# Row corrections of the last four token tiles: from a selecting matmul to rows of x, with the reloads and the tail in another order

## The chip, the cores and the metric

The kernel runs on one core of one Trainium2 chip. The metric is device time in microseconds (us), taken as the median over runs. A profiled execution gives a trace; its span runs from the first to the last instruction of the program, and times inside it are counted from its start.

## The reference

Three things are added for an input x of 2048 tokens by 512 channels, all of them on or from the layer-normed x:

```python
xn = _layernorm(x, axis=-1)
return x + A(xn) + B(xn)

# A: a long convolution, one kernel K of length 2048 per channel
P = exp(dt*A * l);  K = einsum("dn,dnl,dn->dl", C, P, dt*B).real
y = irfft(rfft(xn, 4096) * rfft(K, 4096))[:2048] + xn * Dskip
# B: a gated MLP, 512 -> 1792 -> 512
h = sigmoid(xn @ w_gate) * (xn @ w_up);  return h @ w_down
```

## The kernel before

Channels lie in two halves of 256 (p = 0 and 1), tokens in 16 tiles of 128 rows (i = 0 to 15). The MLP takes four groups of four tiles; jj is the tile in its group, so group 3 holds tiles 12 to 15. The convolution is worked on a 64 by 32 grid: forward transforms, a product per channel and frequency (VectorE, L916 and L920), a back transform (TensorE, L935) whose result V is evacuated by ScalarE (L288) and stored to HBM in the scratch tensors v_scr. After that V is needed in another layout, so it is read back: `reload` has three parts. Part 0 (the first half of the channels, v_scr_99 in the rows of the order, `v_scr0` in the code) comes in four pieces of 512 KB; part 1 (v_scr_100, three quarters of the second half) in four pieces of 384 KB; part 2 (v_scr_101, the last quarter) in four pieces of 128 KB, of which the odd ones go out on ScalarE's DMA queue and the others on SyncE's:

```python
ld = dma("ACT" if n == 2 and k % 2 else "SP", dst, v_v[:, :, w * k:w * (k + 1), :], ...)
```

Piece k serves tiles 4k to 4k+3, that is the tile pairs t = 2k and 2k+1. The last transform, `s2_mm` (L994), takes V to tokens: two column halves of two row halves for each tile, so eight matmuls of 256 columns for a pair and four for a tile.

The tail has two kinds of work. `final(t)`, t = 0 to 5, is for the tiles of the groups 0 to 2, whose MLP and x are already summed: eight matmuls into a pair of PSUM banks, then one VectorE addition of 1024 columns (L1020) and a store. The tiles of group 3 do it in one accumulation: 14 matmuls of the down projection (L1123) into a bank, then the four of `s2_mm` into the same bank, then VectorE adds x from the tile xt (L1143) and the row is stored. The last tile is cut in two column pieces of 256.

The convolution's grid leaves eight late output rows (rows 95 and 127 of the tiles 12 to 15) that lack a term. It is worked out as eight rows of 512 (`f_rz` on VectorE, four transposing matmuls L964, an evacuation by ScalarE at L966 into `rr`) and added by a fifth matmul per tile, L997, with a table of ones, `sr`, that puts each row of `rr` on its place. The other 120 rows of `rr` are set to zero by GpSimd (L854), and `sr` is loaded from a constant (c_SR).

All instructions are recorded as operations and issued in the order of one long list of numbers, `ORDER`; each engine and each DMA queue runs its own in that order, and one that waits holds up all behind it on that engine. SyncE issues nearly all the transfers, ScalarE a few. In the list, 817 to 820, 821 to 824 and 825 to 828 are the four pieces of the parts 0, 1 and 2; 829 + 3t is the matmuls of `final(t)`, 830 + 3t its addition and 831 + 3t its store.

Of the kernel before, what the change touches and what calls it, by code (L numbers as in the profile page):

```python
# [20 lines left out]
D = 512  # L21
# [161 lines left out]
def _consts():  # L183
    S1 = _build_S1()
    M2 = _build_M2()
    MA, MB = _build_MAB()
    by = np.arange(NU).reshape(2, NU // 2).T.reshape(NU)

    def quads(m, cross=False):
        m = m.transpose(1, 0, 2)  # L190
        lo, hi = m[0:64, :, 0:64].copy(), m[64:128, :, 64:128].copy()
        if cross:
            lo[:, 1::2], hi[:, 1::2] = m[64:128, 1::2, 64:128], m[0:64, 1::2, 0:64]
        return np.concatenate([lo, hi], axis=0)

    f = lambda v: np.ascontiguousarray(v.astype(np.float32)).astype(ml_dtypes.bfloat16)
    sr = np.zeros((128, 4, 64))
    for q in range(8):
        sr[q, q // 2, 31 + 32 * ((q ^ (q // 2)) % 2)] = 1.0
    return dict(SR=f(sr), ident=f(np.eye(128)), S1=f(np.tile(S1, (4, 1))), S2=f(np.stack([_build_S2(by), np.roll(_build_S2(by), 32, axis=1)], axis=1)), M2=f(quads(M2[by])),  # L200
                MAB=f(np.stack([quads(MA[by], True), quads(MB[by], True)], axis=2)), E=f(_build_E(M2, by).reshape(128, NU // 2, 2, NKT, 128).transpose(1, 0, 2, 3, 4)))
# [117 lines left out]
def kernel(  # L319
# [25 lines left out]
    def bank(slot, r=0):  # L345
        if slot.pool == "s":
            return pairs[slot.idx][:, 512 * r:512 * r + 512]
        return banks[slot.idx][:]
# [53 lines left out]
    sr = at(OFF["tmp"] + 3 * KB // 2, [4, 64])  # L402
# [449 lines left out]
    l_sr = load("SP", sr, cten["SR"].ap(), 64 * KB, deps=table_free, pkt=512)  # L852
    l_s2 = load("SP", s2, cten["S2"].ap(), 32 * KB, deps=table_free, pkt=256)
    m_rr = pl.add("POOL", 0.3, lambda: P.memset(rr, 0.0), table_free, 60)  # L854
# [97 lines left out]
    def f_rz():  # L952
        ka, kb_ = k2[:, 0:KT].unsqueeze(2), k2[:, KT:2 * KT].unsqueeze(2)
        V.tensor_tensor(out=rf[:, :, 0:4], in0=pre[:], in1=kb_.to_broadcast([128, KT, 4]), op=ALU.mult)
        V.tensor_tensor(out=rf[:, :, 4:6], in0=pre2[:], in1=ka.to_broadcast([128, KT, 2]), op=ALU.mult)
        V.tensor_tensor(out=rz[:, :, 4:8:2], in0=pre[:, :, 0:2], in1=ka.to_broadcast([128, KT, 2]), op=ALU.mult)
        V.tensor_copy(out=rz[:, :, 1:4:2], in_=rf[:, :, 0:2])
        V.tensor_tensor(out=rz[:, :, 5:8:2], in0=rf[:, :, 2:4], in1=rf[:, :, 4:6], op=ALU.add)
# [7 lines left out]
    o_rz = pl.add("ACT", 0.48, lambda slr=slr: S.activation(out=rr[0:8, :], in_=bank(slr)[0:8, :], func=ACT.Identity), [o_rt, l_sr, m_rr], 60, rel=[slr])  # L966
# [21 lines left out]
    def s2_mm(t, r, o, start, w):  # L988
# [7 lines left out]
        if i >= 12:  # L996
            T.matmul(o[64:128, :], sr[:, i - 12, :], rr[:, w[0]:w[1]], start=False, tile_position=(0, 64), **kw)  # L997
# [27 lines left out]
    for grp in range(4):  # L1025
# [77 lines left out]
        for jj in range(4):  # L1103
# [3 lines left out]
            if jj == 0:  # L1107
                if late:
                    xt = at(TAIL["xt"], [4, D])
                    lx = [dma("SP", xt, xv[:, i:i + 4, :], deps=[prods[0]] + table_free, prio=3,  # L1110
                              pkt=4096)(512 * KB)]
            last = late and jj == 3
# [3 lines left out]
            ver = vp_op[i // 2] + [l_s2, o_rz]  # L1116
# [96 lines left out]
```

## Time and profile before

| | |
|---|---|
| median of 3 runs | 214.91 us (214.5 to 215.3) |
| profiled execution, span | 213.6 us |
| median less that span | 1.3 us |
| busy: TensorE, VectorE, ScalarE, GpSimd | 204.2, 191.3, 177.1, 27.8 us |
| granted TensorE clock | 1.000 |
| HBM read, written | 24.99 MB, 12.85 MB |

No device time of its own is shown for the profiled execution beside its span, so durations of the trace are set against the 213.6 us, and the 1.3 us that lie around it go unchanged to the median. In the rows below PE is TensorE, DVE VectorE, ACT ScalarE, POOL GpSimd and SP SyncE; a q behind an engine marks what its sequencer issues, a DMA for instance. "big" is the one SBUF tile in which most buffers lie, pair and bank are PSUM. A row of the timeline gives start, length, engine, line, operation, output and inputs, shape and count, and in brackets the idle time ahead and what ended it. Some matmul records are missing (a down projection of 14 stands with 13 in one row).

### The profile page before, as it was taken

The page shows a single profiled execution, that of the slowest core. Times are in us where ns is not written, and L with a number is a line of the kernel's source. Part 1 is how long each engine was busy: PE and PEld are TensorE (multiplying, and loading weights), DVE is VectorE, ACT ScalarE, POOL GpSimd, SP SyncE. Part 2 cuts the span into 40 slices and gives each one's busy share as a digit, 9 for nine tenths or more (in the row PEclk, how much of TensorE's full clock was granted, in tenths as well). Part 3 has the DMA queues.
Part 4 walks back from the last instruction along what each step waited for, and adds up shares of the span by engine and source line. Part 5 has one row for each costly group of instructions (what it writes and reads, how often), then busy time and mean ns, then how long its engine had stood idle before and what let it go on. Part 6 is the DMA issues. An engine that isn't in the chain of part 4 may idle for free.

```text
span 213.6 us, 4875 instructions
## 1 busy us (share of the span) xinstructions
PE 204.2 (96%) x1838; PEld 102.9 (48%) x1864; DVE 191.3 (90%) x406; ACT 177.1 (83%) x284; POOL 27.8 (13%) x32
## 2 busy tenths in 40 slices
PE   7989999999999999999999999999999999999992
PEld 2654444444443444445436555544654645644482
DVE  4799999999979999999999999999992999990494
ACT  5699999999999999997999989978989998870000
POOL 2120026008980000002000000001200000000000
PEclk9999999999999999999999999999999999999999
DMA  5999269124464236967965878787967799698864
GB/s 148 316 383 381 100 147 324 61 98 147 110 126 104 76 105 229 213 191 151 249 185 141 228 202 237 215 221 175 202 188 208 217 284 274 141 357 218 240 213 172
DMA packets 52377, 42.61 MB, mean 199 GB/s; under 512 B 16641, under 2 KB 44546, under 8 KB 52354
## 3 DMA queue, kind: packets, MB, share of 16 engines
q1 hardware_dynamic: 50658, 40.30, 63.9%
q0 software_dynamic: 864, 1.57, 4.8%
q10 hardware_dynamic: 832, 0.43, 0.8%
q8 instruction: 14, 0.23, 0.5%
q14 instruction: 9, 0.07, 0.1%
HBM read 24.99 MB, written 12.85 MB: 177 GB/s over the span
## 4 chain that ended last, share of the span: by engine, by line
PE 41%; DVE 40%; POOL 6%; DMA 4%; issue 4%; ACT 3%; DVEq 0%; SPq 0%; ACTq 0%
PE pair L911 8%; PE bank L1045 7%; PE bank L1123 7%; PE bank L1069 7%; DVE big L737 6%; DVE big L738 6%; POOL ln_ve_b L481 5%; PE pair L935 5%; DVE big L742 4%; DVE big L743 4%; DVE stats L542 3%; DVE hT_sb L1094 3%; DVE hT_sb L1089 3%; DVE big L678 2%; DMA big<-v_scr 2%
## 5 line engine op out<-in xcount | busy, mean ns | idle before, releaser
L288 ACT ACTIVATE big<-pair 128x1024 bf16<-128x1024 f32 x64 | 64.5, 1039 | 6.9 <-DVE big L920 1.7
L1069 PE MATMUL bank<-xnT,wu_sb 128*128 128x512 bf16 x214 | 52.9, 379 | 1.7 <-issue 0.6
L1123 PE MATMUL bank<-wd_sb,hT_sb 128*128 128x512 bf16 (+1 forms) x231 | 50.6, 367 | 0.5 <-issue 0.2
L1045 PE MATMUL bank<-xnT,wg_sb 128*128 128x512 bf16 (+1 forms) x191 | 45.6, 370 | 1.0 <-issue 0.5
L1045 PEld LDWEIGHTS <-wg_sb 128*128 128x128 bf16 x240 | 22.5, 98 | 25.0 <-issue 3.2
L1123 PEld LDWEIGHTS <-hT_sb 128*128 128x128 bf16 x238 | 22.4, 98 | 24.9 <-issue 1.6
L1069 PEld LDWEIGHTS <-wu_sb 128*128 128x128 bf16 x224 | 20.7, 98 | 27.5 <-issue 5.4
L1057 ACT ACTIVATE hT_sb<-bank 128x512 bf16<-128x512 f32 x48 | 28.2, 627 | 0.7 <-PE bank L1045 0.7
L737 DVE TENSOR_TENSOR big<-big 128x1024 bf16<-128x1024 bf16 (+4 forms) x40 | 26.7, 667 | 0.2
L738 DVE TENSOR_TENSOR big<-big 128x1024 bf16<-128x1024 bf16 (+4 forms) x40 | 26.5, 663 | 0.0
L1084 ACT ACTIVATE us_sb<-bank 128x512 bf16<-128x512 f32 x40 | 23.6, 616 | 0.6 <-DVE hT_sb L1089 0.3
L911 PE MATMUL pair<-big 128*128 128x256 bf16 x160 | 19.8, 273 | 0.0
L916 DVE TENSOR_TENSOR big<-big 128x2048 bf16<-128x2048 bf16 x16 | 19.3, 1217 | 0.1
L911 PEld LDWEIGHTS <-big 128*128 128x128 bf16 x160 | 15.4, 98 | 4.7 <-issue 0.8
L481 POOL TENSOR_SCALAR ln_ve_b<-mvb 128x4 bf16<-128x4 bf16 x3 | 13.0, 4323 | 34.1 <-DVE mvb L543 34.1
L742 DVE TENSOR_TENSOR big<-big 128x512 bf16<-128x512 bf16 (+4 forms) x40 | 16.5, 413 | 0.2
L743 DVE TENSOR_TENSOR big<-big 128x512 bf16<-128x512 bf16 (+4 forms) x40 | 16.5, 412 | 0.0
L792 ACT ACTIVATE sq_sb<-big 128x256 bf16<-128x256 bf16 (+2 forms) x20 | 13.2, 658 | 1.6 <-DVE big L743 1.5
L1089 DVE TENSOR_TENSOR hT_sb<-hT_sb,us_sb 128x1024 bf16<-128x1024 bf16 x20 | 13.5, 683 | 0.0
L935 PE MATMUL pair<-big 64*64 64x512 bf16 (+1 forms) x256 | 13.1, 327 | 0.0
L898 DVE COPY big<-big 32x1024 bf16<-32x1024 bf16 x20 | 8.4, 418 | 4.5 <-ACT big L288 4.2
L288 ACT ACTIVATE big<-big 128x256 bf16<-128x256 bf16 x30 | 12.4, 452 | 0.0
(99 smaller groups left out, 229.8 us busy)
## 6 DMA issues: line engine op xcount, KB each, us to landing
big<-c_E SPq DMA_DIRECT2D x13, 320.0 KB, 4.4
z_scr<-big SPq DMA_DIRECT2D x16, 256.0 KB, 2.9
big<-z_scr SPq DMA_DIRECT2D x16, 256.0 KB, 4.2
v_scr<-big SPq DMA_DIRECT2D x16, 256.0 KB, 3.2
big<-big SPq DMA_DIRECT2D x44, 64.0 KB, 3.3
big<-in_A_u_dram SPq DMA_DIRECT2D x4, 512.0 KB, 9.1
wu_sb<-in_B_w_up_dram SPq DMA_DIRECT2D x2, 896.0 KB, 10.8
wd_sb<-in_B_w_down_dram SPq DMA_DIRECT2D x1, 1792.0 KB, 9.0
```

Of the source, the lines that this page charges most:

```text
L288: nc.scalar.activation(out=get(out), in_=get(in_), func=ACT.Identity)
L481: P.tensor_scalar(out=q["ve_b"], in0=mvb[:, s, 1], scalar1=EPS, scalar2=None, op0=ALU.add)
L737: V.tensor_tensor(out=wide(outp), in0=wide(lo), in1=mre, op=ALU.mult)
L738: V.tensor_tensor(out=wide(tb()), in0=wide(lo), in1=mim, op=ALU.mult)
L742: V.tensor_tensor(out=outp[:, :, 0], in0=outp[:, :, 0], in1=tb()[:, :, 1], op=opr)
L743: V.tensor_tensor(out=outp[:, :, 1], in0=outp[:, :, 1], in1=tb()[:, :, 0], op=opi)
L911: T.matmul(two(sk)[:, o:o + DW], es()[:, g, kt, :], kTv[p][:, :, kt, :], start=kt in (0, NKT - 1), stop=kt >= NKT - 2)
L935: T.matmul(two(sv)[o:o + 64, DW * (2 * g + y):2 * DW * (g + 1)], mab[b:b + 64, 2 * u + g, q, :], pq()[b:b + 64, q, ch] if y else pp()[b:b ...
L1045: T.matmul(bank(sl, k % 2)[:, c0:c1], w[:, kt, k * 128:(k + 1) * 128], xnT[:, grp, kt, c0:c1], start=(kt == 0), stop=(kt == KT - 1))
L1057: S.activation(out=hT_sb[:, hs.idx, k % 2, :], in_=bank(sl), func=ACT.Sigmoid)
L1069: T.matmul(bank(sl), wu_sb[:, kt, k * 128:(k + 1) * 128], xnT[:, grp, kt, :], start=(kt == 0), stop=(kt == KT - 1))
L1123: T.matmul(bank(po)[:, 0:c[1] - c[0]], hT_sb[:, hts[k // 2].idx, k % 2, jj * 128:(jj + 1) * 128], wd_sb[:, k, c[0]:c[1]], start=first and ...
```

## The change

The eight corrections no longer go through TensorE at the end. The eight rows of x concerned are loaded beside (x8, two transfers of 4 KB), VectorE adds them to the corrections as it evacuates them into `rr` (in ScalarE's place), and two transfers of 4 KB on ScalarE's queue write the sums over the same rows of xt, after xt itself has landed. The matmul L997, the table `sr` with its 64 KB load, and the memset of `rr` go. The columns of `rz` are numbered otherwise, to suit the two transfers. `ORDER` is another list from its second half on:

```diff
-    l_sr = load("SP", sr, cten["SR"].ap(), 64 * KB, deps=table_free, pkt=512)
+    l_x8 = [load("SP", x8[b:8:2, :], xv[95 + 32 * b, 12:16, :], 4 * KB, deps=table_free, pkt=1024) for b in range(2)]
     l_s2 = load("SP", s2, cten["S2"].ap(), 32 * KB, deps=table_free, pkt=256)
-    m_rr = pl.add("POOL", 0.3, lambda: P.memset(rr, 0.0), table_free, 60)
...
-    o_rz = pl.add("ACT", 0.48, lambda slr=slr: S.activation(out=rr[0:8, :], in_=bank(slr)[0:8, :], func=ACT.Identity), [o_rt, l_sr, m_rr], 60, rel=[slr])
+    o_rz = pl.add("DVE", 0.61, lambda slr=slr: V.tensor_tensor(out=rr[0:8, :], in0=bank(slr)[0:8, :], in1=x8[0:8, :], op=ALU.add), [o_rt] + l_x8, 60, rel=[slr])
...
-        if i >= 12:
-            T.matmul(o[64:128, :], sr[:, i - 12, :], rr[:, w[0]:w[1]], start=False, tile_position=(0, 64), **kw)
...
                     lx = [dma("SP", xt, xv[:, i:i + 4, :], deps=[prods[0]] + table_free, prio=3,
                               pkt=4096)(512 * KB)]
+                    lx = [dma("ACT", xt[95 + 32 * b:96 + 32 * b, :, :], rr[b:8:2, :], deps=lx + [o_rz], prio=3, pkt=1024)(4 * KB) for b in range(2)]
...
-            ver = vp_op[i // 2] + [l_s2, o_rz]
+            ver = vp_op[i // 2] + [l_s2]
```

Three places show how the list moves the tail. First SyncE's queue, from its last loads of the table E on. v_scr_99, _100 and _101 are the parts 0, 1 and 2 of V: an arrow from them is a reload, an arrow to them a store; the 128x2048 from in_A_u_dram is xt. Before:

```order
L422 DMA k_93<-c_scr 128x8x1
L422 DMA v_scr_100<-big 128x4x256
L422 DMA big<-in_A_u_dram 128x2048
L422 DMA big<-v_scr_99 128x2x1024
L422 DMA xnT<-v_scr_99 128x2x1024
L422 DMA v_scr_101<-big 128x4x256 x2
L422 DMA big<-v_scr_100 96x2x1024
L422 DMA big<-v_scr_101 32x2x1024
L422 DMA big<-v_scr_100 96x2x1024 x3
L422 DMA out_dram<-big 128x1024
```

Now:

```order
L421 DMA k_93<-c_scr 128x8x1
L421 DMA xnT<-v_scr_99 128x2x1024
L421 DMA v_scr_100<-big 128x4x256 x2
L421 DMA big<-v_scr_99 128x2x1024
L421 DMA big<-in_A_u_dram 128x2048
L421 DMA v_scr_101<-big 128x4x256 x2
L421 DMA big<-v_scr_100 96x2x1024 x3
L421 DMA big<-v_scr_101 32x2x1024 x2
L421 DMA big<-v_scr_100 96x2x1024
L421 DMA out_dram<-big 128x1024 x4
```

A reload of part 0 stands ahead of two stores of part 1, and the load of xt behind them; three reloads of part 1 stand ahead of those of part 2, which have to wait for the two stores of part 2 just above. By the list, the first of the three is now piece 1, then 3, then 0; before it was 0, and behind the reload of part 2's piece 0 came 3, 1 and 2.

Second the end of ScalarE's list, whose DMAs are the pieces 3 and 1 of part 2, in this order before and now. Before:

```order
L1057 ACTIVATE hT_sb<-bank_67 128x512
L966 ACTIVATE big<-pair_63 8x512
L422 DMA big<-v_scr_101 32x2x1024 x2
L422 DMA out_dram<-big 128x256
L1209 UNCONDITIONAL_BRANCH
```

Now:

```order
L1053 ACTIVATE hT_sb<-bank_68 128x512
L287 ACTIVATE big<-pair_63 128x1024
L421 DMA big<-v_scr_101 32x2x1024 x2
L421 DMA big<-big 1x4x512 x2
L421 DMA out_dram<-big 128x256
```

The evacuation of the eight rows has left ScalarE, and the two row transfers into xt stand behind the two reloads.

Third TensorE after the down projections of jj = 0 and 1 (banks 68 and 67). A pair is a `final`; rows that repeat are left out. Before, the finals are those of t = 1 and then t = 0:

```order
L994 MATMUL pair_63<-big 64x256
...
L1123 MATMUL bank_65<-wd_sb,hT_sb 128x512
...
L994 MATMUL bank_68<-big 64x256
...
L997 MATMUL bank_68<-big 64x512
...
L994 MATMUL bank_67<-big 64x256
```

Now they are t = 3 and then t = 2:

```order
L992 MATMUL pair_63<-big 64x256
...
L992 MATMUL bank_68<-big 64x256
...
L992 MATMUL bank_67<-big 64x256
...
L1120 MATMUL bank_66<-wd_sb,hT_sb 128x512
...
L992 MATMUL bank_66<-big 64x256
```

The last transform of jj = 0 and 1 stands ahead of the down projection of jj = 2 (bank 65 before, bank 66 now) and no longer behind it. VectorE's additions keep their sequence of shapes: two of 1024, three of 512, two of 1024, one of 256, two of 1024, one of 256; the first two now serve t = 3 and 2, the next two t = 1 and 0, the last two t = 5 and 4.

More of the change, by code (lines that the diff above doesn't have):

```diff
@@ L196, in _consts @@
     f = lambda v: np.ascontiguousarray(v.astype(np.float32)).astype(ml_dtypes.bfloat16)
[L197 to L200, printed above, removed]
+    return dict(ident=f(np.eye(128)), S1=f(np.tile(S1, (4, 1))), S2=f(np.stack([_build_S2(by), np.roll(_build_S2(by), 32, axis=1)], axis=1)), M2=f(quads(M2[by])),
                 MAB=f(np.stack([quads(MA[by], True), quads(MB[by], True)], axis=2)), E=f(_build_E(M2, by).reshape(128, NU // 2, 2, NKT, 128).transpose(1, 0, 2, 3, 4)))
@@ L401 @@
     rr = at(OFF["tmp"] + KB // 2, [D])
-    sr = at(OFF["tmp"] + 3 * KB // 2, [4, 64])
+    x8 = at(OFF["tmp"] + 2 * KB, [D])
     W = [at(OFF["W%d" % p], [12, 2, DW]) for p in range(NP)]
@@ L955, in f_rz @@
         V.tensor_tensor(out=rf[:, :, 4:6], in0=pre2[:], in1=ka.to_broadcast([128, KT, 2]), op=ALU.mult)
-        V.tensor_tensor(out=rz[:, :, 4:8:2], in0=pre[:, :, 0:2], in1=ka.to_broadcast([128, KT, 2]), op=ALU.mult)
-        V.tensor_copy(out=rz[:, :, 1:4:2], in_=rf[:, :, 0:2])
-        V.tensor_tensor(out=rz[:, :, 5:8:2], in0=rf[:, :, 2:4], in1=rf[:, :, 4:6], op=ALU.add)
+        V.tensor_tensor(out=rz[:, :, 4:8:3], in0=pre[:, :, 0:2], in1=ka.to_broadcast([128, KT, 2]), op=ALU.mult)
+        V.tensor_copy(out=rz[:, :, 1:3], in_=rf[:, :, 0:2])
+        V.tensor_tensor(out=rz[:, :, 5:7], in0=rf[:, :, 2:4], in1=rf[:, :, 4:6], op=ALU.add)
     o_rz = pl.add("DVE", 0.95, f_rz, [k_l, o_pre], 60)
```

82 rows, old and new, of the table ORDER are left out of this document.

## The prediction

> **What bounds the kernel now.** I began with the page: how long the span is, where VectorE and the DMA engines stand in its 40 slices (5.34 us each), and how the chain that ended last is shared out.
>
> ```profile
> span 213.6 us, 4875 instructions
> DVE  4799999999979999999999999999992999990494
> DMA  5999269124464236967965878787967799698864
> PE 41%; DVE 40%; POOL 6%; DMA 4%; issue 4%; ACT 3%; DVEq 0%; SPq 0%; ACTq 0%
> ```
>
> VectorE is full almost everywhere up to slice 35 and has one hole near the end, the digits 0 and 4. The chain spends only 4% on DMA, so one should see where. The chain of waits over the last 28 us (start, length, what):
>
> ```profile
> 191.27 2.59 DMA v_scr<-big
> ...
> 193.92 4.70 DMA big<-v_scr
> ...
> 198.67 0.95 PE pair L994 x14
> 199.62 0.16 issue
> 199.78 2.97 PE bank L1123 x13
> 202.75 0.44 PE bank L994 x5
> 203.20 0.12 PE bank L997
> 203.32 0.02 issue
> 203.34 0.69 DVE big L1143
> ...
> 204.60 0.52 DVE big L1143
> ```
>
> The last store of part 2 of V, then its reload (825, piece 0), then at 198.67 the finals of t = 1 and 0 on TensorE, then the down projection of jj = 2, and from 203.34 VectorE to the end. The timeline of VectorE shows the hole itself:
>
> ```profile
> 190.86 1.87 DVE L1094 TENSOR_TENSOR hT_sb<-hT_sb,bank 128x512 bf16<-128x512 bf16 x3
> 199.23 2.36 DVE L1020 TENSOR_TENSOR big<-pair,glu_sb 128x1024 bf16<-128x1024 f32 x2 [6.50 <-PE pair L994]
> 203.34 1.94 DVE L1143 TENSOR_TENSOR big<-bank,big 128x512 bf16<-128x512 f32 x3 [1.76 <-PE bank L997]
> 205.20 2.34 DVE L1020 TENSOR_TENSOR big<-pair,glu_sb 128x1024 bf16<-128x1024 f32 x2
> 207.47 0.41 DVE L1143 TENSOR_TENSOR big<-bank,big 128x256 bf16<-128x256 f32 x1
> 207.80 2.34 DVE L1020 TENSOR_TENSOR big<-pair,big 128x1024 bf16<-128x1024 f32 x2
> 210.06 0.41 DVE L1143 TENSOR_TENSOR big<-bank,big 128x256 bf16<-128x256 f32 x1
> ```
>
> VectorE waits 6.50 us for the first final and 1.76 us for the first tile of group 3, and then works without a gap to 210.47. So the end is set by the moment S at which the first final finds all its pieces (198.67), by the hole of 1.76, and by a fixed rest. TensorE's timeline says what it had before S:
>
> ```profile
> 197.13 1.03 PE L1123 MATMUL bank<-wd_sb,hT_sb 128*128 128x512 bf16 x4
> 198.09 0.30 PE L994 MATMUL pair<-xnT,big 128*64 128x256 bf16 x2
> 198.67 0.30 PE L994 MATMUL pair<-big 128*64 128x256 bf16 x2 [0.28 <-DMA big<-v_scr]
> ```
>
> The down projections of jj = 0 and 1 end at 198.1 to 198.2, so TensorE itself could begin at 198.2 and the reload costs half a microsecond. The transfers around it, by issue (the queue of ScalarE sends two reloads, 828 and then 826; the three rows behind it are its first, its second and SyncE's 825; then SyncE's first of 384 KB and its last two), KB each and us to landing:
>
> ```profile
> 194.01 1.43 ACTq L422 DMA_DIRECT2D big<-v_scr  x2
> ...
> big<-v_scr ACTq DMA_DIRECT2D x1, 128.0 KB, 4.8
> ...
> big<-v_scr ACTq DMA_DIRECT2D x1, 128.0 KB, 5.6
> ...
> big<-v_scr SPq DMA_DIRECT2D x1, 128.0 KB, 4.7
> ...
> big<-v_scr SPq DMA_DIRECT2D x1, 384.0 KB, 4.3
> ...
> big<-v_scr SPq DMA_DIRECT2D x2, 384.0 KB, 7.1
> ```
>
> **The change part by part.** The order decides most. The first finals are now t = 3 and 2, which read piece 1. Its last quarter is 826, the second reload on ScalarE's queue. That queue still waits for both stores of part 2, so the issue stays where it was: 194.01 for 828, half of 1.43 us later, 194.7, for 826. Before, 826 landed 5.6 us later, at 200.3, and nobody needed it then. Now TensorE stands at it, and with it everything behind in its list.
>
> *After S.* Call S' the first matmul that needs 826. VectorE starts 0.56 us behind it (198.67 to 199.23) and does two additions of 1024 in 2.36 us: free at S' + 2.92. Before, it then waited for jj = 0, whose transform stood behind the down projection of jj = 2. Now the transforms of jj = 0 and 1 stand ahead of it. The 16 matmuls of two finals take 0.95 us, so these eight take about 0.48; they are done by S' + 1.5, and VectorE goes on at once with two additions of 0.65 (1.94 / 3): busy to S' + 4.2. TensorE goes on with the down projection of jj = 2 (0.16 + 2.97) and its four matmuls with the handing over (0.44 + 0.02): 0.95 + 0.48 + 3.13 + 0.46 = S' + 5.02. There the third addition starts. Before, it started at 204.60, that is S + 5.93, and from it on both kernels have the same shapes on VectorE. Gain of the order: 5.93 - 5.02 = 0.91 us, call it 0.9; the hole shrinks from 1.76 to 0.8. The L997 matmuls that go are in this figure (0.12 on the chain).
>
> *S' itself.* If 826 lands as before, S' is 200.31 + 0.05 = 200.36: +1.69 us. The nearest rows bound it: no earlier than TensorE is free, 198.2 (-0.47); no later than the longest reload here, 7.1 us, from 194.7: 201.8 (+3.2). Two things pull. Three reloads of 384 KB now go ahead of the stores' landing, where one went: more is in the queue before 826. But the engines also had room:
>
> ```profile
> 194.00:196.00 2.00, 2.00 (x11) 0.87 (x9) 0.00 (x0) 0.00 (x0) 0.00 (x0) 1.00 0.70 210
> 196.00:198.60 2.60, 2.39 (x12) 0.89 (x10) 0.00 (x0) 0.00 (x0) 0.00 (x0) 1.00 0.93 240
> ```
>
> (stretch, its length, busy time of TensorE, weight loads, VectorE, ScalarE and GpSimd, clock, DMA share, GB/s.) In the two microseconds behind the stores the share is 0.70; the new order fills them with work that before was done later. And what stood right beside 826, the second reload of 384 KB, has moved ahead of it, not vanished. I take 200.3, the old landing, with up to 1.5 us on top in the rival below.
>
> *The row transfers.* Their price isn't in the trace; the nearest rows are a small transfer to HBM, the load of xt, which they follow, and the two stores of part 2, ahead of which xt is now issued:
>
> ```profile
> c_scr<-k_scr SPq DMA_DIRECT2D x1, 1.0 KB, 4.8
> ...
> big<-in_A_u_dram SPq DMA_DIRECT2D x1, 512.0 KB, 5.7
> ...
> 190.35 1.27 SPq L422 DMA_DIRECT2D v_scr<-big  x2
> ```
>
> They are issued behind the reloads, at 195.4 and 196.1 (0.72 us each, as these). xt goes out before 190.35 and is there by 196.05 at 5.7 us, so it holds them little. At 4.8 us, or the 5.6 of the reload ahead of them, the last is there between 200.9 and 201.7; the addition that reads it starts at S' + 2.92 = 203.3. Hidden by 1.6 us; without that cover each microsecond of lateness counts in full. Behind them on ScalarE's queue there is only the last output.
>
> *The evacuation.*
>
> ```profile
> 192.10 0.59 ACT L966 ACTIVATE big<-pair 8x512 bf16<-8x512 f32 x1 [0.37 <-PE pair L964]
> 165.21 0.55 SPq L422 DMA_DIRECT2D big<-c_SR  x1
> ```
>
> ScalarE's 0.59 us becomes an addition of VectorE of some 0.65 (the same 512 columns from PSUM). VectorE idles 6.50 us there; even ahead of its last products it delays them to 193.4, and the down projection of jj = 2 that needs them starts at 199.78. Nothing, and 0.65 if that hole were gone. The memset goes from GpSimd, which the chain of the tail never meets. The one load of 64 KB becomes two of 4 KB: one issue more on SyncE, 0.55 us, around 165, ahead of transfers between the halves of the grid. Between 0 and 0.55; I take 0, since VectorE has copies and products of other channels to do there.
>
> *Other moves on SyncE.* xt and a reload of part 0, 512 KB each, change places; if xt collides with the last stores, it shows in S' (each 0.1 us that they land later is 0.1 us for 826), and stays within its bounds. Piece 2 of part 1 is now the last of its queue; its tiles, t = 5 and 4, are the last pair of additions, 207.80 before. At the end the list puts a 256 KB store just before the last one:
>
> ```profile
> 210.50 0.38 ACTq L422 DMA_DIRECT2D out_dram<-big  x1
> ...
> out_dram<-big SPq DMA_DIRECT2D x1, 256.0 KB, 2.1
> out_dram<-big ACTq DMA_DIRECT2D x1, 64.0 KB, 2.0
> ```
>
> Such a store stood 0.33 us ahead of it before too (2.1 and 2.0 us, both landed by 212.5). I take 0, at most +0.3.
>
> **Sum.** On the profiled execution: 213.6 + 1.69 (S') - 0.9 (order) = 214.4; all else 0. The median is 1.3 above that span, so 214.91 + 0.8 = 215.7 us. The bounds of S' give 214.91 - 0.47 - 0.9 = 213.5 and 214.91 + 3.2 - 0.9 = 217.2.
>
> **Rivals.** First, *slower, by arrival order.* If the DMA engines serve the transfers in the order in which they are issued, 826 stands behind and within 3 x 384 + 4 x 128 = 1664 KB, where it stood within 2 x 384 + 3 x 128 = 1152. The other 512 KB take 2.1 us at the 240 GB/s of the row above; the room of 194 to 196, 0.3 x 2.0 = 0.6 us, comes off. 826 lands at 201.8, S' is 201.85, and the time is 214.91 + 3.18 - 0.9 = 217.2. For it: before, the landings keep the order of issue by and large (825 at 198.62, 828 at 198.8, 826 at 200.3), and the last two of 384 KB took 7.1 us where the first took 4.3. Against: the surplus was issued from 191.8 on, and much of it is through by the time 826 comes. Where S' passes 200.6, the change is slower by more than 0.5%.
>
> Second, *faster, by a fair share between the queues.* If ScalarE's queue gets its turn beside SyncE's, whatever is queued there, its 256 KB need half of 240 GB/s from 194.01: 2.1 us, and some 2 us that even a lone 64 KB store takes here. That is 198.2, TensorE never waits, S' is 198.2 and the time is 213.5. Speaking for it is that 826 was issued behind 384 KB on SyncE's queue that took longer than it; against it that 828 needed 4.8 us, as long as SyncE's 825 beside it, where a turn of its own would have brought it at 197.1. [...]
>
> Third, *a new wait for the row transfers.* It decides only if S' is early: with S' = 198.2 the addition wants them at 201.1, and at 5.6 us they come at 201.7, so 213.5 becomes 214.1. It is a case within the second, and takes something from it. At S' = 200.4 they would need 7.2 us from 196.1, above every small row shown.
>
> **How the numbers follow.** Within 0.5% means within 1.07 us of 214.91, about what a measurement of this kernel can tell from no change. My forecast (826 between 199 and 200.6, times from 214.3 to 215.9) has 0.43. Arrival order, 217.2, and mixtures of the two above 215.98, have 0.35. The fair share, 213.5, with its own wait for the rows above it, has 0.20; what is left, 0.02, is that something upstream of 190 moved, to either side. Faster by over 0.5% needs S' below 198.5: 0.20. Slower: 0.37. Same: 0.43. The range, both bounds of S', is 213.5 to 217.2; the likeliest case alone is 214.3 to 215.9.
>
> **What would show it.** In the changed profile, the first final's matmul (L992) should be idle before for a DMA big<-v_scr and start at 200.4, with VectorE's hole ahead of it 7 to 8 us; a start at 201.8 is arrival order, one at 198.2 with no wait the fair share. VectorE's second hole should be 0.8 us, behind two additions of 512 columns and not ahead of three; if it is still 1.8, the order did nothing. The addition of jj = 0 should follow without a wait; one for a DMA big<-big is the third rival. If the products end later than 193.5, or the stores of part 2 land after 194.3, my premise that the stage ahead stays as it was is wrong, and with it the sum.

## The result, and the profile after

The changed kernel takes 221.06 us (median of 4 runs, 218.96 to 221.84), the kernel before 214.7 beside it. The ratio is 1.028, with a 95% interval of 1.0222 to 1.0338: slower by about 6 us, where I forecast 215.7 and a range of 213.5 to 217.2. The profiled execution took 220.75 us and has a span of 218.9, 5.3 more than the one of before. Ratios leave out runs that lie more than 1.5% above the fastest of their kernel; there were two of these, among the ten of the kernel with both late orders undone.

The page after, the same rows (TensorE's clock beside them):

```profile
span 218.9 us, 4896 instructions
DVE  3799999999979999999999999999929999940664
PEclk9999999999999999999999999999999999999699
DMA  5999269024654157779577779688875899798226
```

VectorE's hole near the end has grown, and TensorE's clock has a 6 in it that before had only nines. The chain of waits over the end:

```profile
193.05 7.08 DMA big<-v_scr
...
200.15 3.41 DMA big<-v_scr
203.56 1.69 PE pair L992 x14
205.25 0.85 PE bank L992 x8
206.10 3.32 PE bank L1120 x14
209.42 0.36 PE bank L992 x4
...
209.80 0.03 DVE big L1140
```

Ahead of the finals there is now only waiting for V. (The view puts the last wait down to the reload issued at 200.15, SyncE's piece 2 of part 1, which these finals don't read and which landed at 204.47; what they wait for is 826, which landed at 203.41.) Behind them in TensorE's list stands the down projection of jj = 2, whose last product VectorE ended at 193.17; it starts at 206.03. The finals that took 0.95 us take 1.69. TensorE's timeline at that place:

```profile
192.51 6.22 PE L1120 MATMUL bank<-wd_sb,hT_sb 128*128 128x512 bf16 x28
198.66 0.30 PE L992 MATMUL pair<-xnT,big 128*64 128x256 bf16 x2
203.54 0.42 PE L992 MATMUL pair<-big 128*64 128x256 bf16 x2 [4.58 <-DMA big<-v_scr]
```

and VectorE's:

```profile
204.49 2.36 DVE L1016 TENSOR_TENSOR big<-pair,glu_sb 128x1024 bf16<-128x1024 f32 x2 [10.72 <-issue]
206.76 1.28 DVE L1140 TENSOR_TENSOR big<-bank,big 128x512 bf16<-128x512 f32 x2
209.80 0.69 DVE L1140 TENSOR_TENSOR big<-bank,big 128x512 bf16<-128x512 f32 x1 [1.76 <-PE bank L992]
```

The profiled executions enter the tail at different times (from 190.7 to 192.5 us), for reasons ahead of what is changed there: the changed kernel and the one that only swaps 826 and 828 are 1.7 us apart already at the start of the down projection of jj = 0 (192.51 and 190.85). So all that follows is counted from F, the start of the down projection of jj = 0 and 1, and from S, the first matmul that needs the last piece of V. Before, F was 191.94 and S was F + 6.73; now F is 192.51 and S is F + 11.03. Before, the third addition of 512 started at S + 5.93; now at S + 6.26.

### The profile page after: what moved, and what is told of

It reads as the page before. It is cut to its first block, busy times and chain, and to the rows that moved or that the text cites. A ratio compares the mean times of both kernels' runs of the same rounds, so it can differ in the third digit from the quotient of the medians.

```text
span 218.9 us, 4896 instructions
## 1 busy us (share of the span) xinstructions
PE 206.2 (94%) x1859; PEld 102.8 (47%) x1859; DVE 191.8 (88%) x407; ACT 176.4 (81%) x283; POOL 27.4 (13%) x31
## 5 line engine op out<-in xcount | busy, mean ns | idle before, releaser
L1065 PE MATMUL bank<-xnT,wu_sb 128*128 128x512 bf16 x224 | 54.0, 380 | 0.7 <-ACT hT_sb L1053 0.2
L1120 PE MATMUL bank<-wd_sb,hT_sb 128*128 128x512 bf16 (+1 forms) x238 | 51.3, 368 | 0.0
L1041 PE MATMUL bank<-xnT,wg_sb 128*128 128x512 bf16 (+1 forms) x200 | 46.9, 371 | 0.5 <-ACT xnT L571 0.5
L1016 DVE TENSOR_TENSOR big<-pair,glu_sb 128x1024 bf16<-128x1024 f32 x4 | 4.7, 1217 | 10.7 <-issue 10.7
L541 DVE BATCH_NORM_STATS2 stats<-big 128x6 f32<-128x512 bf16 x15 | 9.8, 679 | 3.4 <-DMA big<-in_A_u_dram 3.4
```

Source lines behind the costliest of these rows:

```text
L1041: T.matmul(bank(sl, k % 2)[:, c0:c1], w[:, kt, k * 128:(k + 1) * 128], xnT[:, grp, kt, c0:c1], start=(kt == 0), stop=(kt == KT - 1))
L1065: T.matmul(bank(sl), wu_sb[:, kt, k * 128:(k + 1) * 128], xnT[:, grp, kt, :], start=(kt == 0), stop=(kt == KT - 1))
L1120: T.matmul(bank(po)[:, 0:c[1] - c[0]], hT_sb[:, hts[k // 2].idx, k % 2, jj * 128:(jj + 1) * 128], wd_sb[:, k, c[0]:c[1]], start=first and ...
```

## The experiments

My theory after the result: 826 lands late because of its place in the queues and because of the volume ahead of it, and TensorE's clock falls in the wait. Rivals: the row corrections cost the time; the new order of the tail does; or the landing is late whatever is ahead.

### The volume alone, in the kernel before

```diff
-908, 821, 911, 825, 832, 833, 829, 828, 824, 826, 915, 909, 921, 822, 823,
+908, 821, 911, 824, 822, 825, 832, 833, 829, 828, 826, 915, 909, 921, 823,
```

> The kernel before with one edit: the reloads 824 and 822 (384 KB each) ahead of 825 on SyncE's queue, nothing else. If the volume ahead is the cause, 825 lands about 3.3 us later (202 instead of 198.6), TensorE stands for 3.5 us or more, its clock falls, and the time rises by 3 to 4.5 us, to 218 to 219. If the corrections, the finals or the tail's order are the cause, it stays within 1 us of 214.7.

Measured 219.65 us, ratio 1.023 (1.019 to 1.027), somewhat above the 219 that I expected; all four runs lie above 218.9, and all 13 of the kernel before below 215.7. TensorE, in that kernel:

```profile
202.34 0.39 PE L994 MATMUL pair<-big 128*64 128x256 bf16 x2 [3.91 <-DMA big<-v_scr]
```

S is F + 10.36 (F is 191.98): 3.6 us later, by two reloads of 384 KB and nothing else. 768 KB in 3.6 us are 0.21 KB per ns. This one edit makes the kernel before about as slow as the whole change does.

### The row corrections alone, in the order of before

The changed code, with the list of the kernel before (numbers from 908 on are two higher there, and 372 and 373 have changed places), and the two row transfers behind 826:

```diff
-888, 880, 908, 821, 911, 825, 832, 833, 829, 828, 824, 826, 915,
+888, 880, 910, 821, 913, 825, 832, 833, 829, 828, 824, 826, 909, 908, 917,
```

> The changed kernel's corrections (x8, the addition on VectorE, two row transfers into xt) in the order of the kernel before, reloads, finals and tail as there. My price for them was nothing: 214.7, within 0.5. If the row transfers or the addition on VectorE cost time, more than 0.5 us above 214.7.

Measured 215.06 us against 214.96, ratio 1.0003 (0.9983 to 1.0023). On balance they cost nothing and bring nothing. Both sides are small here; they come apart further down.

### 826 ahead of 828

```diff
-828, 863, 826, 822, 887,
+826, 863, 828, 822, 887,
```

> The changed kernel with the two reloads on ScalarE's queue in the other order: 826, for which the first finals wait, before 828. Arrival order: 826 takes the place of 828, which landed 1.0 us earlier (202.40 against 203.41); the first finals start about 1.0 us earlier and the time falls to about 220.0. A late landing that does not depend on what is queued ahead: no change, 221.

Measured 219.4 us (218.01 to 220.06), ratio 1.0205 (1.0159 to 1.0252). TensorE:

```profile
200.27 0.30 PE L990 MATMUL pair<-big 128*64 128x256 bf16 x2 [2.97 <-issue]
202.61 0.85 PE L990 MATMUL bank<-big 128*64 128x256 bf16 x6 [1.10 <-DMA big<-v_scr]
203.40 5.38 PE L1118 MATMUL bank<-wd_sb,hT_sb 128*128 128x512 bf16 x14
```

The two changed places with the issues, as arrival order says: the finals, which read 826, go on at 200.27, and the transforms of jj = 0 and 1, which read 828, stand for a reload until 202.61, where in the changed kernel 828 landed 1.0 us ahead of 826. S is F + 9.42, 1.6 us earlier. But the 14 matmuls of the down projection of jj = 2 took 5.38 us where they take some 3.2, so most of that went again. In the windows of this kernel the clock is still whole at S and then half for nearly 7 us (stretch, length, busy TensorE, weight loads, VectorE, ScalarE, GpSimd, granted clock, DMA share, GB/s):

```profile
200.00:201.00 1.00, 0.73 (x14) 0.76 (x16) 0.11 (x1) 0.00 (x0) 0.00 (x0) 1.00 1.03 162
201.00:202.00 1.00, 0.51 (x7) 0.07 (x2) 1.00 (x1) 0.00 (x0) 0.00 (x0) 0.51 0.68 137
...
206.00:207.00 1.00, 1.00 (x4) 0.39 (x3) 0.00 (x0) 0.00 (x0) 0.00 (x0) 0.50 0.03 8
207.00:208.00 1.00, 1.00 (x4) 0.33 (x3) 0.00 (x0) 0.00 (x0) 0.00 (x0) 0.57 0.00 0
```

### SyncE's reloads as before, in the changed kernel

A first try put pieces of part 2 in front, but left 824 and 821 behind matmuls that read them in the list. So the transforms of jj = 0 and 1 take what lies in the buffer ahead of their piece of V, and this kernel's time says nothing; only what lies ahead of them can be read.

```diff
-826, 822, 887, 888, 875, 876, 601, 824, 602, 909, 908, 910, 913, 838, 835, 911, 914, 839, 836, 912, 821, 915, 825, 827,
+826, 822, 887, 888, 875, 876, 601, 825, 602, 909, 908, 910, 913, 838, 835, 911, 914, 839, 836, 912, 827, 915, 824, 821,
```

> The changed kernel with SyncE's reloads in the order 822, 825, 827, 824, 821, 823: only one transfer of 384 KB ahead of the pieces of part 2 instead of three. Arrival order: 826 lands near 200 instead of 203.4, TensorE waits little, so its clock stays at 1.0 and the finals take 0.95 us again instead of 1.69; the time falls by 3.5 to 5 us to 216 to 217.5, unless 824, which jj = 0 and 1 need, now comes late by up to 1 us. A fair share between the queues, with a landing set by something else: about 221 as before.

Measured 219.23 us, not to be compared. With one reload of 384 KB ahead, and 824 sent only after the finals, S is F + 6.78 (F is 190.78):

```profile
197.56 0.30 PE L990 MATMUL pair<-big 128*64 128x256 bf16 x2 [0.32 <-DMA big<-v_scr]
...
206.34 0.30 PE L990 MATMUL pair<-big 128*64 128x256 bf16 x2 [2.56 <-DMA big<-v_scr]
```

The second row, a wait far behind them, is for the section on the hardware.

The next one has all reloads ahead of their readers:

```diff
-826, 822, 887, 888, 875, 876, 601, 824, 602,
+826, 822, 825, 824, 827, 821, 887, 888, 875, 876, 601, 602,
...
-912, 821, 915, 825, 827, 917,
+912, 915, 917,
```

> The changed kernel with SyncE's reloads sent as before: 822, then 825 of part 2, then 824, 827, 821, all ahead of their readers in the list; the corrections, the finals' order (t = 3 and 2 first) and the new tail stay. If the volume ahead of 826 and the clock that falls in the wait are the whole loss, 826 lands some 5 us after its issue, the first finals start about 8 us after the down projection of jj = 0 (11.0 in the changed kernel, 6.7 before), the clock stays near 1.0, and the time is 215 to 216.5. If the finals' order or the tail costs something of its own, it stays above 217.

Measured 217.39 us (216.22 to 218.85), ratio 1.0152 (1.0091 to 1.0213). TensorE, then VectorE:

```profile
200.84 0.30 PE L990 MATMUL pair<-big 128*64 128x256 bf16 x2 [2.33 <-DMA big<-v_scr]
```

```profile
205.74 0.69 DVE L1138 TENSOR_TENSOR big<-bank,big 128x512 bf16<-128x512 f32 x1 [0.74 <-PE bank L990]
```

S is F + 8.78, 2.25 earlier than in the changed kernel, where I expected about 8. The third addition starts at S + 4.90, and the clock of this execution is 1.0. So the tail does what I wrote: 5.93 has become 4.90. The median is above the 216.5 that I expected: two of its four runs have a lower mean clock, 0.992, and take 218.07 and 218.85, the other two 216.22 and 216.71. It is above 217 too, which I had said would mean a cost of the finals' order or of the tail; the profiled tail shows none. The wait of 2.33 us left the clock at 1.0 in this execution.

### Work for TensorE in the wait

The first build had its extra matmuls in all four groups, by a slip:

> The changed kernel with 20 more matmuls of the down projection of jj = 1 (its first 6, then all 14, whose sums the 14 that count overwrite), 4.4 us of TensorE's work in the wait for 826. They add nothing to the path if the wait is 4.6 us. If the fallen clock (0.50 from 203.4 to 206.2) comes from the wait, it stays at 1.0, the two finals take 0.95 us and not 1.69, and the time falls by about 1.2 us to 219.8. If the clock falls for another reason, or costs nothing, it stays at 221 or rises.

Measured 232.93 us, ratio 1.0871 (1.0835 to 1.0906); three of four lots lay on the path far ahead of the tail. In the tail itself the third addition of 512 started 4.28 us behind the first final's addition (217.69 and 221.97), where the changed kernel has 5.31, and the clock of all four runs is 1.0. The build for group 3 alone:

```diff
+            more = list(range(6)) + list(range(FT)) if grp == 3 and jj == 1 else []
-            def fd(jj=jj, po=pos[0], c=cols[0], hts=hts, first=not last):
-                for k in range(FT):
+            def fd(jj=jj, po=pos[0], c=cols[0], hts=hts, first=not last, ks=more + list(range(FT))):
+                for k in ks:
```

> The changed kernel with 20 more matmuls of the down projection of jj = 1 in group 3 alone (their sums are overwritten by the 14 that count): 4.4 us of TensorE's work in the wait for 826. If the fallen clock (0.50 from 203.4 to 206.2 in the changed kernel) comes from the wait, it stays at 1.0, the third addition of 512 starts 4.9 us after the first finals and not 6.3, and the time falls by 1.4 us to 219.7. If the wait is not the reason: 221.

Measured 218.57 us (217.62 to 220.07), ratio 1.0185 (1.011 to 1.026): 20 matmuls more, and 2.5 us less. TensorE, then VectorE:

```profile
190.78 10.53 PE L1120 MATMUL bank<-wd_sb,hT_sb 128*128 128x512 bf16 x48
202.31 0.30 PE L990 MATMUL pair<-big 128*64 128x256 bf16 x2 [0.77 <-DMA big<-v_scr]
```

```profile
207.21 0.69 DVE L1140 TENSOR_TENSOR big<-bank,big 128x512 bf16<-128x512 f32 x1 [0.74 <-PE bank L990]
```

The third addition is at S + 4.90 again, although S is as late as ever (F + 11.53). With 0.77 us left of the wait of 4.58 the clock is 1.0 from 198 to 205, where the changed kernel falls to 0.50; that is 6.26 - 4.90 = 1.36 us in the profiled tail. The medians differ by more than that. Part of the rest may be the clock too, for two of the changed kernel's four runs have a mean clock of 0.981 and 0.982, against 0.992 in the profiled one and 0.997 to 1.0 with the extra matmuls; how much is scatter of the landing, I can't say.

### Both late orders undone

```diff
-828, 863, 826, 822, 887, 888, 875, 876, 601, 824, 602,
+826, 863, 828, 822, 825, 824, 827, 821, 887, 888, 875, 876, 601, 602,
...
-912, 821, 915, 825, 827, 917,
+912, 915, 917,
```

> The changed kernel with SyncE's reloads sent as before (822, 825, 824, 827, 821) and, in addition, 826 ahead of 828 on ScalarE's queue: both late orders undone, the corrections, the finals' order and the tail kept. By the volume ahead, 826 lands like 825 of the kernel before, the finals start 6.7 to 7.2 us after the down projection of jj = 0; the transforms of jj = 0 and 1 may wait up to 1 us for 824 and 828. Time 214 to 215.2, and under 214.2 if these come in time.

Measured 215.61 us (214.76 to 219.47), ratio 1.0036 (0.9999 to 1.0074), above the 215.2 that I allowed. S is F + 6.28, without a wait. What comes next, on TensorE and on VectorE:

```profile
199.99 0.52 PE L990 MATMUL bank<-big 128*64 128x256 bf16 x6 [1.82 <-DMA big<-v_scr]
```

```profile
201.89 1.29 DVE L1138 TENSOR_TENSOR big<-bank,big 128x512 bf16<-128x512 f32 x2 [1.81 <-DMA big<-big]
```

Two new waits have taken the place: the transforms of jj = 0 and 1 stand for their pieces (824, 828) by 1.82 us, and the addition of jj = 0 for the row transfers.

### The tail's order alone, in the kernel before

```diff
-824, 826, 915, 909, 921, 822, 823, 830, 831, 827, 912, 916,
+824, 826, 909, 912, 915, 921, 822, 823, 830, 831, 827, 916,
```

> The kernel before with one edit: the last transforms of jj = 0 and 1 ahead of the down projection of jj = 2. My sum put a gain of 0.9 us on this order, 213.8. But without the early reload of piece 3 (824 landed at 200.65 in the kernel before, the transforms would start at 199.6) TensorE should stand 1.0 us at it: then VectorE's wait moves ahead of jj = 0, jj = 2 comes at the old time, and the time stays at 214.7 to 215.2.

Measured 217.4 us (215.66 to 218.64), ratio 1.0144 (1.0082 to 1.0205), worse than the 215.2 that I allowed. TensorE:

```profile
201.33 0.41 PE L994 MATMUL bank<-big 128*64 128x256 bf16 x3 [2.12 <-DMA big<-v_scr]
```

It stands 2.12 us for piece 3, twice what I took from one execution's landing. So the order of the tail and the early reloads are one bargain: the order needs piece 3 early, and with 824 and 822 sent early, in the first experiment, the piece of part 2 behind them came late (S 3.6 us later).

### The gain without the bargain

The transforms of jj = 0 and 1 go in the middle of the down projection of jj = 2, in the kernel before; no transfer moves:

```diff
+            cut = 8 if grp == 3 and jj == 2 else FT
-            def fd(jj=jj, po=pos[0], c=cols[0], hts=hts, first=not last):
-                for k in range(FT):
+            def fd(jj=jj, po=pos[0], c=cols[0], hts=hts, first=not last, ks=range(cut)):
+                for k in ks:
...
-                    pre_ = [pl.add("PE", 0.44, lambda i=i, po=po, c=c: f2(i, po, c, False), [md] + ver, 30, mode="H")]
+                    f3 = lambda i=i, po=po, c=c, fd=fd, ks=range(cut, FT): (fd(po=po, c=c, ks=ks), f2(i, po, c, False))
+                    pre_ = [pl.add("PE", 0.44, f3, [md] + ver, 30, mode="H")]
-915, 909, 921, 822, 823, 830, 831, 827, 912, 916,
+915, 909, 912, 921, 822, 823, 830, 831, 827, 916,
```

> The kernel before with the transforms of jj = 0 and 1 put between the first 8 and the last 6 matmuls of the down projection of jj = 2; no transfer is moved. They start at 201.4, after 824 has landed (200.65), and are done when VectorE has finished the two finals (201.59); jj = 2 follows at 203.6 instead of 204.6. Gain of 0.9 us: 213.8. If a late landing or VectorE's own order eats it: 214.7.

Measured 215.23 us, ratio 1.0034 (1.0008 to 1.0061): no gain, and above both of my values. TensorE:

```profile
199.67 0.52 PE L994 MATMUL bank<-big 128*64 128x256 bf16 x5
199.92 0.38 PE L997 MATMUL bank<-big 128*64 128x512 bf16 x1
...
200.88 1.47 PE L1125 MATMUL bank<-wd_sb,hT_sb 128*128 128x512 bf16 x6
```

The two transforms take 200.88 - 199.67 = 1.21 us with the corrections' matmuls L997 in them. The same split, with the corrections as rows of x (the second kernel above, `cut` 8, and 914 moved ahead of 923):

> The corrections as rows of x in the order of the kernel before, and the transforms of jj = 0 and 1 between the first 8 and the last 6 matmuls of the down projection of jj = 2. No reload moves. Without the matmuls of the corrections the pieces between cost 0.57 us and not 1.21, so the third addition of 512 starts 4.9 us after the first finals (5.9 before): 1.0 us less, 213.9. If the corrections' matmuls cost nothing there, it stays with the same split of the kernel before at 215.2.

Measured 214.65 us (213.86 to 216.27) against 214.92, ratio 0.9998 (0.9965 to 1.0031): the gain of 1.0 us did not come. TensorE, then VectorE:

```profile
194.04 4.71 PE L1120 MATMUL bank<-wd_sb,hT_sb 128*128 128x512 bf16 x21 [0.40 <-DVE hT_sb L1088]
...
201.50 0.76 PE L990 MATMUL bank<-big 128*64 128x256 bf16 x10
202.19 1.47 PE L1120 MATMUL bank<-wd_sb,hT_sb 128*128 128x512 bf16 x6
```

```profile
202.74 1.99 DVE L1141 TENSOR_TENSOR big<-bank,big 128x512 bf16<-128x512 f32 x3 [1.05 <-DMA big<-big]
```

Here the transforms take 202.19 - 201.50 = 0.69 us: a correction by matmul costs 0.26 us a tile where TensorE sets the pace. Two losses eat that: VectorE's addition into rr stands ahead of the last products and holds TensorE by 0.40 us, and the row transfers hold the addition of jj = 0 by 1.05. With the final of t = 3 added into the middle (`cut` 9; 838 ahead of 918, 839 ahead of 919):

> As the one before, with 9 matmuls ahead of the transforms of jj = 0 and 1, the final of t = 3 behind them and its addition ahead of that of jj = 2, so that VectorE has work while TensorE ends the down projection of jj = 2. Its wait there (0.7 us) goes: 213.3. If piece 1 (822) lands after TensorE wants it (202.3 in the kernel before), TensorE stands instead and it is no better than the one before.

Measured 214.63 us and not 213.3, ratio 0.9991 (0.9958 to 1.0023). VectorE's wait only moved, to 1.88 us ahead of jj = 0.

The last two take the two losses away. Both have VectorE's addition into rr (602) behind the last products; one sends the row transfers on GpSimd's queue, the other puts them ahead of 828 and 826:

```diff
-602, 888, 880, 910, 821, 913, 825, 832, 833, 829, 828, 824, 826, 909, 908,
+888, 880, 602, 910, 821, 913, 825, 832, 833, 829, 909, 908, 828, 824, 826,
```

> The split with row corrections in the order of the kernel before, with two edits: the row transfers go out on GpSimd's queue, where nothing is ahead of them, and VectorE's addition into rr stands behind the last two products (in front of them it held TensorE by 0.4 us at 194.0). If the row transfers are what is left of the loss, the wait for big<-big (1.05 us) is gone, jj = 0 is added right behind the finals, and the time falls by 0.5 to 0.9 us to 213.8 to 214.1. If they land as late from there, or TensorE's chain sets jj = 2 anyway: 214.6.

Measured 214.33 us (213.1 to 215.46), ratio 0.9993 (0.997 to 1.0017). The wait for the rows is gone; in the profiled execution 825 came late (TensorE stood 1.00 us for it).

> As the one before, but the row transfers stay on ScalarE's queue, ahead of 828 and 826 instead of behind them. They go out 1.5 us earlier and land about 1.5 us earlier, which is enough for a wait of 1.05 us; 828 and 826 go out 1.2 to 1.8 us later, and 828 is wanted at 201.5. 213.8 to 214.1 if 828 lands in time, 214.6 or more if TensorE then stands for it.

Measured 214.04 us (212.84 to 215.03) against 214.89, ratio 0.9975 (0.9948 to 1.0001), as expected. VectorE:

```profile
198.81 2.35 DVE L1014 TENSOR_TENSOR big<-pair,glu_sb 128x1024 bf16<-128x1024 f32 x2 [5.43 <-PE pair L990]
201.41 1.29 DVE L1141 TENSOR_TENSOR big<-bank,big 128x512 bf16<-128x512 f32 x2 [0.25 <-PE bank L990]
203.48 0.69 DVE L1141 TENSOR_TENSOR big<-bank,big 128x512 bf16<-128x512 f32 x1 [0.78 <-PE bank L990]
```

The additions follow the finals, and the span of this execution is 212.3, 1.3 less than the profiled one of before. By the ratio it is the fastest kernel here, 3% ahead of the change; that it beats the kernel before is likely, but its interval still touches 1.

## Why the prediction was wrong

The likeliest case had the right chain: the first finals stand for 826, and the tail behind them gets shorter. Two terms were missing from it: it put the three reloads ahead of 826 at nothing, and it had no fall of the clock. The two profiled executions differ by 5.3 us, and the runs divide that as follows, each row by a difference of single executions:

| step | forecast | measured | from |
|---|---|---|---|
| 826, not 825, sets S | +1.69 | +2.05 | 8.78 (reloads as before) less 6.73 |
| three reloads of 384 KB ahead | 0 | +2.25 | 11.03 less 8.78 |
| clock in the wait | not seen | +1.36 | 6.26 less 4.90 |
| order of the tail | -0.91 | -1.03 | 4.90 less 5.93 |
| later start of the tail | 0 | +0.57 | F, 192.51 less 191.94 |
| what is left | | +0.1 | |

**The step that failed** is "I take 200.3, the old landing". With SyncE's reloads in their old order that is nearly what comes out (+2.05 for +1.69). With three of them ahead it isn't: S came 2.25 us later still. I argued that "much of it is through by the time 826 comes", and it was not. The issues of the changed kernel, KB and us to landing (824, the second of the three; then 825 and ScalarE's 828; then 826):

```profile
big<-v_scr SPq DMA_DIRECT2D x1, 384.0 KB, 7.1
...
big<-v_scr SPq DMA_DIRECT2D x1, 128.0 KB, 7.3
big<-v_scr ACTq DMA_DIRECT2D x1, 128.0 KB, 7.5
...
big<-v_scr ACTq DMA_DIRECT2D x1, 128.0 KB, 7.8
```

Issued at 193.05, 194.90, 194.92 and 195.61, they land at 200.1, 202.2, 202.4 and 203.4, in the order of issue, whichever queue they are on. My premise that the issue of 828 and 826 "stays where it was" failed too, and with it came the sign that I had named for it, stores of part 2 that land after 194.3: the second landed at 194.82 (193.86 before). The queue that waits for them:

```profile
194.92 1.47 ACTq L421 DMA_DIRECT2D big<-v_scr  x2
```

That is 0.91 us later than the 194.01 of before, of which F makes 0.57. The upper bound of my range rested on the longest reload before, 7.1 us; with three reloads of 384 KB ahead 826 took 7.8 us.

**How much of it is scatter.** The trace keeps sixteen updates of the semaphore for each of these reloads, and TensorE starts behind the last. For 825 in the kernel before the fifteenth comes 3.87 us after the issue and the sixteenth after 4.70 (198.62; S is 198.67), for 826 in the changed kernel after 6.66 and 7.80 us (203.41; S is 203.54). From the fifteenth to the sixteenth of the eight reloads of the parts 1 and 2 it is 0.03 to 0.91 us in the kernel before and 0.35 to 2.15 us in the changed one. So of the 2.25 us at most 1.14, the last update of 826, is such lateness, and 1.1 us or more is not. In the first experiment S is 3.6 us later than before, more than the longest of these gaps, so there it isn't scatter alone, and the runs that the medians stand for don't overlap, neither there (219.65 against 214.96) nor between the changed kernel and the one with SyncE's reloads as before (221.06 against 217.39).

**The first rival** named arrival order and had the sign. I gave it 0.35 and priced 512 KB at 240 GB/s less a gap of 0.6 us: 1.5 us. It was nearer than its 217.2 us says: 826 landed 1.6 us behind the 201.8 that it gave, 0.93 of it by the later issue, and the last update, 1.14 us behind the fifteenth, covers the rest; what it left out is the clock. Two reloads alone cost 3.6 us in the kernel before, which is 0.21 KB per ns. The 240 GB/s that I took were not kept up to the landing of 826; the windows of the changed kernel from TensorE's wait on (columns as in the windows above, GB/s last):

```profile
198.50:201.00 2.50, 0.46 (x4) 0.11 (x2) 0.00 (x0) 0.00 (x0) 0.00 (x0) 1.00 0.93 196
201.00:203.50 2.50, 0.00 (x0) 0.00 (x0) 0.00 (x0) 0.00 (x0) 0.00 (x0) 0.91 0.59 182
```

In the second window the DMA share is 0.59 only: within it 826 got its fifteenth update (202.27), and the last came at 203.41.

The second rival, a fair share, doesn't hold: 828 took 7.5 us beside 825's 7.3. Nor was the order of issue strict between the queues: in the kernel before, 824 (384 KB), issued by SyncE at 194.58, landed at 200.65, behind ScalarE's 826, issued at 194.68 and landed at 200.31. What sets the order between the queues, the runs don't show.

**What no case held** is the clock. Every case of mine that had TensorE wait left its speed as it was. The forecast for the tail's order was right only where the clock stayed up, 4.90 with extra matmuls in the wait or with old reloads, and I had no row for a long wait, since in the tail of the kernel before the longest was 0.28 us.

**The rest, point by point.** The row transfers and VectorE's evacuation show no wait in the change and cost nothing on balance alone (1.0003). The third rival, a wait for the row transfers, came up as soon as S was early: 1.81 and 1.05 us, more than the 0.6 that I had given it. The matmuls L997 were worth more than the 0.12 of the chain: 0.26 us a tile once TensorE, and not VectorE, sets the pace. And of the signs that I named, TensorE's wait and the start of the first final were the right ones to look at (203.54, past the 201.8 that meant arrival order). VectorE's second hole was 1.76 and not 0.8, which I had said would mean that "the order did nothing"; that reading was wrong, since the hole was the slow clock's: 0.74 where the clock was whole. I also put 1.3 us between the span and the time; in the runs with both numbers it is 1.8 (220.75 and 218.9).

With the row corrections alone S was F + 8.4 and the time still that of before: in that execution F was 190.75, 1.2 us earlier than before, and TensorE stood 1.35 us for the reload (S is 199.13); both have a span of 213.6. Not settled is why a last update comes late.

## What to carry to other kernels

The transfers that the end waited for here were priced by what was issued before them, on both queues, and not by their own size (825, 828 and 826, 128 KB each, took 4.7 to 5.6 us to land before and 7.3 to 7.8 us with three reloads of 384 KB ahead); before sending something "early", count the KB that it puts ahead of what is needed first. The waits of 2.56 us and more on TensorE were paid twice here, the second time in the matmuls behind them (1.36 us in the changed kernel). Before a difference of 1 to 2 us is read out of two single executions, look whether a late last update of one transfer makes it (up to 2.15 us behind the fifteenth in the changed kernel). And when an order shortens the tail, ask which pieces it needs sooner: here the gain of 1.0 us was real, but the transfers that made it possible cost more than it.

## What the runs showed of the hardware

In four of the executions profiled TensorE's granted clock dropped to half around the end of a wait of 2.56 us or more, and stayed there for 3.4 to 6.8 us, whatever work had come by then. The windows of the changed kernel, with the same columns as above:

```profile
202.00:203.00 1.00, 0.00 (x0) 0.00 (x0) 0.00 (x0) 0.00 (x0) 0.00 (x0) 1.00 0.90 281
203.00:204.00 1.00, 0.46 (x6) 0.48 (x8) 0.00 (x0) 0.00 (x0) 0.00 (x0) 0.52 0.21 59
204.00:205.00 1.00, 1.00 (x12) 0.99 (x10) 0.51 (x1) 0.00 (x0) 0.00 (x0) 0.50 0.06 16
...
206.00:207.00 1.00, 1.00 (x6) 0.44 (x5) 1.00 (x2) 0.00 (x0) 0.00 (x0) 0.77 0.40 147
```

Four microseconds of waiting pass at 1.0; the drop falls at about 203.0, 0.5 us ahead of the wait's end, and half of the clock lasts to 206.5, for 3.4 us by these windows. Behind the wait of 3.91 us (two reloads ahead, in the kernel before) it lasted 3.4 us as well, from 202.4 to 205.8. Behind that of 2.56 us (the first try with SyncE's reloads) 14 matmuls of 256 columns took 2.79 us, where the changed kernel's at 210.67 took 1.70, and the mean clock of 0.992 over the span of 217.1 us makes some 3.5 us of half speed. With the wait of 2.97 us it lasted from 201.0 to 207.9 (6.8 us), beginning 0.8 us after TensorE was at work again; a second wait, of 1.10 us, lies inside it. Waits of 2.12 and 2.33 us left the clock at 1.0 in the windows of the executions profiled, and not in all runs: with 2.33 us in the profiled one, the two runs at a mean clock of 0.992 took some 2 us more than the two at 1.0. How long the wait was in each of those runs, no trace shows, nor does any run show what sets when the drop comes and how long it lasts.

In the changed kernel a reload of 384 KB (822) had fifteen of its sixteen updates 3.98 us after its issue and the last at 6.13 us, and one of 128 KB (826) 6.66 and 7.80 us after it; the first matmul that needs 826 starts 0.13 us behind its last.
